# A routing search with its grids made in one instruction, and a weight's low half moved from TensorE and ScalarE to GpSimd

## The chip, the cores and the metric

The kernel runs on one core of a Trainium2 chip. The metric is the device time of one execution in microseconds. The engines are TensorE (PE in the rows; its weight loads are PEld), VectorE (DVE), ScalarE (ACT), GpSimd (POOL) and SyncE (SP), which issues most of the DMAs.

## The reference, cut to what matters

Three stages follow one another: attention that keeps the 32 best scores of a row, a mixture of eight experts with a capacity, and a rational activation between two products.

```python
def _moe_ref(x, w_gate, w1, w2):          # x: 2304 tokens x 512
    cap = N // E                          # 288 tokens for each of E = 8 experts
    logits = x @ w_gate
    order = np.argsort(-logits.flatten())
    for idx in order:                     # the best (token, expert) pairs first
        tok, e = int(idx) // E, int(idx) % E
        if assigned[tok] >= 0 or counts[e] >= cap:
            continue
        assigned[tok] = e
        counts[e] += 1
    ...
    for e in range(E):
        mask = assigned == e
        h = np.maximum(x[mask] @ w1[e], 0.0)
        out[mask] = h @ w2[e]

def _moe2_ref(x, w_in, w_out, a, b):
    h = x @ w_in
    P = a[0] + a[1] * h + a[2] * h**2 + a[3] * h**3
    Q = 1.0 + np.abs(b[0]) * np.abs(h) + np.abs(b[1]) * h**2
    return (P / (Q + 1e-06)) @ w_out
```

## The kernel before

**Stages.** The first 460 us are attention, 72 units of 128 rows by two heads, in an order written out by hand. Then comes routing, then the experts, eight in turn, each with two products (w1, w2) and the two of the rational stage (w_in, w_out).

**Weights.** The large products run in three half-precision passes, so every weight is split into a high half and a low half (`w1s`, `w2s`, `win`, `wout`). For w_in and w_out this takes several instructions: ScalarE makes "heads" (`heads`, L374 to L386), VectorE puts in the mantissa and the sign (`signed` L396, `mantissa` L409, `apply_sign` L413, in pieces of 256 columns), ScalarE sums squares (`square`, L307), and once a block's scale is known ScalarE makes the high half (L437) and VectorE the low one (L441). For the first expert's w1 and w2 (`add_first`) ScalarE makes the high half in four pieces of 1024 columns (`conv_hi`, L1361). The low half comes 256 columns at a time: TensorE multiplies the raw weights with a diagonal matrix that holds the scale (L1425) and subtracts the high half (L1426), and ScalarE copies the sum out of PSUM (L1429). There are 16 such pieces for w1 and 16 for w2. When the last is done, `stage` lets SP load four more raw pieces of w_out into the place that held the raw weights.

**Routing.** `route` replaces the sort by seven searches; each finds a threshold `edge` above which the next expert (or experts) fill up. A search has `ITS` = 4 iterations on a grid of `GR` = 32 thresholds, each grid 32 times finer than the last. In an iteration VectorE compares the 18 x 128 token values `vt` with the 32 thresholds `thr`, in two halves (`cmp`, L1493). TensorE counts how many tokens of each expert lie above each threshold, with 18 matmuls (L1501) and one for the need row (L1499, L1509 in the first iteration). VectorE makes `over`, which marks thresholds whose count reaches the need (L1565). TensorE adds `over` over the 32 thresholds and spreads the sum to all partitions (`pt`, L1569). VectorE makes the next grid from it:

```python
low = thr[:, 0:1] - step[:, it]                   # L1555, under the counts
nxt = iota_r * step[:, it + 1] + low              # L1558, under the counts
thr = step[:, it] * pb[:, 0:1] + nxt              # L1577, after the sum
```

After the fourth iteration VectorE makes `full` (which experts are full, L1582) and `edge` (L1583), masks the logits (`lc`, L1698), marks the tokens above the edge (`gone`, L1650) and starts the next search with `rng` (L1529) and its first grid `thr` (L1533). GpSimd multiplies the one-hot choice with `gone` (`asel`, or `asg` the first time; `give`, L1656), TensorE counts that with 18 matmuls (L1659), and the count goes into the `need` of the next search (L1671). GpSimd adds `asel` to `asg` (L1677).

**The order of the work around it.** Everything else is put between these instructions by a planner, `Flow`. It has a task for each piece of weight work, with an engine, a cost, the tasks that it needs and a rank. It keeps a clock for each engine and starts the task that can start first, ties by rank. `fill(n)` gives VectorE tasks of up to n us at a place in the program, and ScalarE, GpSimd and DMA tasks that by its clock start within 1.5 us (`LA`) of VectorE's. `tail(n)` gives TensorE up to n tasks. In each iteration there is a `fill` of 0.6 us under the counts (`J1`, `J3`), a `tail` of one task after the sum and a `fill` of 0.37 us (`J2`); between two searches a `tail` of one and a `fill(J4)` of 0. At the start of a search's last iteration GpSimd's clock is set 4.5 us ahead:

```python
if it == ITS - 1:
    flow.free["G"] = max(flow.free["G"], flow.free["V"] + 4.5)
```

No task on GpSimd was in those places before: `flow.add("G", ...)` stood only for the loads of an expert's rows and for the stores. Each engine runs its own instructions in program order and waits only for what they need.

After routing, `slots` and `rows_of` work out which rows go to which expert, a check sets a flag, and rows are gathered. If the flag is set, routing and all experts are run a second time by a slower path.

Of the kernel before, what the change touches and what calls it, by code (L numbers as in the profile page):

```python
# [8 lines left out]
F32 = mybir.dt.float32  # L9
BF16 = mybir.dt.bfloat16  # L10
# [5 lines left out]
OP = mybir.AluOpType  # L16
# [13 lines left out]
class Flow:  # L30
# [69 lines left out]
    def use(self, cost):  # L100
        self.free["V"] += cost
        return self.free["V"]
# [77 lines left out]
class Mark:  # L180
    end = None
# [3 lines left out]
def kernel(  # L185
# [62 lines left out]
    nc.vector.memset(onesb, 1.0)  # L248
    ones_row = consts.tile([1, P], F32, name="ones_row")
    nc.vector.memset(ones_row, 1.0)  # L250
    coef = consts.tile([P, 16], F32, name="coef")
# [11 lines left out]
    nc.gpsimd.iota(iota_r, pattern=[[1, GR]], base=0, channel_multiplier=0, allow_small_or_imprecise_dtypes=True)  # L263
    iota_f = consts.tile([P, GR], F32, name="iota_f")
    nc.vector.tensor_scalar(iota_f, iota_r, 1.001 / GR, None, op0=OP.mult)
    ITS, ITS_SLOW = 4, 7
    fine = consts.tile([P, ITS_SLOW], F32, name="fine")
    fine_slow = consts.tile([P, ITS_SLOW], F32, name="fine_slow")
    for i in range(ITS_SLOW):
        nc.vector.memset(fine[:, i : i + 1], 1.001 / GR ** (i + 1))  # L270
        nc.vector.memset(fine_slow[:, i : i + 1], 1.0 / (GR - 2) ** (i + 1))
# [204 lines left out]
    with ExitStack() as actx:  # L476
# [921 lines left out]
        def stage(which):  # L1398
# [11 lines left out]
            for i in range(4):  # L1410
                fetch((t[:, 1024 * i : 1024 * (i + 1)], -1, after), NP - 8 + 4 * (which - 1) + i)

        def add_first(which):

            scaled = add_steps(scale_steps(which, 0), [], -90.0)
            diag = npool.tile([P, P], F32, name=f"diag{which}", bufs=1)
            copies = [flow.add("A", 0.1, lambda: nc.scalar.activation(
# [40 lines left out]
        def routing(x, xs, lg, span, fast):  # L1458

            with ExitStack() as rctx:  # L1460
# [61 lines left out]
                def first_grid(slow, top):  # L1522

                    step = rw.tile([P, ITS_SLOW], F32, name="step")
                    rng = rw.tile([P, 1], F32, name="rng")
                    thr = rw.tile([P, GR], F32, name="thr")

                    def begin():
                        nc.vector.tensor_scalar(rng, top, span[:, 0:1], 1e-30, op0=OP.subtract, op1=OP.max)  # L1529

                    def middle():
                        if not slow:
                            nc.vector.tensor_scalar(thr, iota_f, rng, span[:, 0:1], op0=OP.mult, op1=OP.add)  # L1533

                    def end():
                        nc.vector.tensor_scalar(step, fine_slow if slow else fine, rng, None, op0=OP.mult)

                    return step, thr, begin, middle, end

                def search(edge, grid, vt, oh, need, fill, tail, use, until):  # L1540

                    step, thr = grid[0:2]
                    for it in range(ITS):
# [3 lines left out]
                        if it == 0:  # L1547
                            grid[4]()
                            need, rest = need()
                            compare(pc, need)  # L1550
                            rest()
                            use(0.4)
                        counts = use(C1) + 0.6
                        low = rw.tile([P, 1], F32, name="low")
                        nc.vector.tensor_tensor(low, thr[:, 0:1], step[:, it : it + 1], op=OP.subtract)  # L1555
                        if it < ITS - 1:
                            nxt = rw.tile([P, GR], F32, name="nxt")
                            nc.vector.tensor_scalar(  # L1558
                                nxt, iota_r, step[:, it + 1 : it + 2], low, op0=OP.mult, op1=OP.add
                            )  # L1560
                        use(0.28)
                        fill(J1 if it else J3)
                        until(counts)
                        over = rw.tile([GR, E + 1], BF16, name="over8")
                        nc.vector.tensor_scalar(  # L1565
                            over[:, 1:], pc, 0.0, None, op0=OP.is_ge, op1=OP.max, accum_out=over[:, 0:1]
                        )
                        pb = psr.tile([P, 512], F32, name="pt")[:, 0 : E + 1]
                        nc.tensor.matmul(pb, onesb[0:GR, :], over, start=True, stop=True)  # L1569
                        sums = use(0.07) + 0.36  # L1570
# [948 lines left out]
```

## Time and profile before

| | |
|---|---|
| three runs | 1209.81, 1213.32, 1213.90 us; median 1213.32 us |
| profiled execution | 1213.61 us, its span 1211.7 us |
| busy share of the span | PE 92%, DVE 87%, ACT 84%, POOL 32% |
| TensorE's mean granted clock | 0.929 |

Shares are averages over stages with different limits. The times below count from the first instruction of the profiled execution. Attention ends at about 460 us, the searches run to 545, slots and the gather to about 560, and the experts run to the end. In a row of the timeline the first number is the start, the second the duration in microseconds, then the engine, the line, the operation, what is written and read, the shapes, how many instructions the row stands for, and in brackets how long the engine had been idle before and what ended that.

### The profile page before, as it was taken

To read this page: it belongs to the slowest core of one execution; us is meant where nothing else is said; L and a number is where in the kernel's file an instruction comes from. 1 tells how busy PE (TensorE), PEld (TensorE's weight loads), DVE (VectorE), ACT (ScalarE), POOL (GpSimd) and SP (SyncE) were. 2 spreads that over 40 slices of the span, in tenths; PEclk is the share of its full clock that TensorE was granted. 3 is DMA by queue.
4 is the path that set the end of the run, shared out by engine and by line. 5 is a ranking of instruction groups with operands and counts; after the bars stand their busy time and mean duration, and the time that the engine had idled before them with its cause. 6 is when DMAs were issued, how large, how long until landed. Compare 5 with 4: busy or idle time off the path is not lost.

```text
span 1211.7 us, 26863 instructions
## 1 busy us (share of the span) xinstructions
PE 1117.0 (92%) x9716; PEld 903.7 (75%) x9716; DVE 1053.6 (87%) x4093; ACT 1020.0 (84%) x1816; POOL 385.3 (32%) x488
## 2 busy tenths in 40 slices
PE   5899999999999887885769999999999999999996
PEld 3688888888888765654546778888888888888774
DVE  5999999989889947888899789898989899897795
ACT  4999999999999796579999888888889888875684
POOL 3788888878777600003000010110100110001010
PEclk8899999999999985555989999999999999999998
DMA  5205102112000307412241302221311222000000
GB/s 126 52 10 160 45 22 52 27 44 52 2 2 2 140 1 289 150 54 89 72 159 71 139 27 84 90 90 71 98 51 52 90 90 84 8 1 21 1 22 22
DMA packets 81246, 80.62 MB, mean 67 GB/s; under 512 B 59984, under 2 KB 60112, under 8 KB 81104
## 3 DMA queue, kind: packets, MB, share of 16 engines
q1 hardware_dynamic: 78032, 69.34, 18.2%
q0 software_dynamic: 3072, 9.48, 2.7%
q8 instruction: 78, 1.28, 0.4%
q14 instruction: 64, 0.52, 0.1%
HBM read 69.25 MB, written 9.55 MB: 65 GB/s over the span
## 4 chain that ended last, share of the span: by engine, by line
PE 71%; DVE 14%; ACT 9%; issue 2%; POOL 1%; DMA 1%; SPq 0%; POOLq 0%; DVEq 0%; ACTq 0%
PE po L887 9%; PE s L696 6%; PE pt L855 5%; PE po L2017 4%; PE po L2018 4%; PE po L2016 4%; PE ph L2016 4%; PE pa L2016 4%; PE ph L2018 4%; PE ph L2017 4%; PE pa L2018 4%; PE pa L2017 4%; PE pt L859 3%; PE po L891 2%; PE pl L1425 2%
## 5 line engine op out<-in xcount | busy, mean ns | idle before, releaser
L789 POOL TENSOR_TENSOR win<-sv,sg 128x576 f32<-128x576 f32 x142 | 179.1, 1282 | 64.4 <-ACT sg L784 47.2
L753 DVE MAX8 cd<-sv 128x8 f32<-128x82 f32 (+1 forms) x1008 | 178.1, 229 | 11.0 <-ACT sv L706 10.9
L2016 PE MATMUL ph<-x,win 128*128 128x288 f16 x512 | 148.3, 290 | 7.6 <-DVE uv L2285 7.5
L887 PE MATMUL po<-vm,pT 128*128 128x65 f32 (+1 forms) x1280 | 152.4, 267 | 2.1 <-issue 1.1
L2017 PE MATMUL po<-g,wout 128*128 128x288 f16 x512 | 146.4, 286 | 2.3 <-DVE g L2007 2.3
L2017 PE MATMUL ph<-x,win 128*128 128x288 f16 x512 | 148.3, 290 | 0.0
L2018 PE MATMUL ph<-x,win 128*128 128x288 f16 x512 | 148.1, 289 | 0.0
L2016 PE MATMUL po<-g,wout 128*128 128x288 f16 x512 | 146.4, 286 | 1.4 <-ACT g L2006 1.3
L2018 PE MATMUL po<-g,wout 128*128 128x288 f16 x512 | 146.4, 286 | 0.0
L887 PEld LDWEIGHTS po<-vm,pT 128*128 128x128 f32 (+1 forms) x1280 | 140.2, 183 | 5.1 <-issue 2.1
L855 PE MATMUL pt<-ident,sv 128*128 128x128 f32 x648 | 125.8, 283 | 0.3 <-ACT pT L869 0.3
L859 PE MATMUL pt<-dg,mk 128*128 128x128 bf16 x720 | 120.0, 220 | 1.2 <-POOL mk L846 1.2
L1993 POOL DMA_INDIRECT xe<-xrows,rows_i x24 | 28.5, 1189 | 286.2 <-PE pa L2028 266.0
L2276 ACT ACTIVATE z<-ph,inv 128x288 f32<-128x288 f32 x128 | 63.6, 497 | 57.9 <-PE ph L2018 54.9
L784 ACT ACTIVATE sg<-sv,cut_all 128x576 bf16<-128x576 f32 x142 | 109.0, 777 | 3.8 <-DVE cut_all L759 3.8
L2406 POOL DMA_INDIRECT out_dram<-ob,tok x21 | 23.2, 1105 | 277.2 <-ACT ob L2402 223.0
L845 ACT ACTIVATE sg<-sv,pn 128x576 bf16<-128x576 f32 x136 | 97.8, 770 | 13.5 <-POOL pn L823 13.5
L696 PE MATMUL s<-region 64*128 64x288 f32 (+1 forms) x640 | 95.3, 451 | 13.1 <-ACT region L667 9.0
L790 DVE MAX8 w<-win 128x8 f32<-128x576 f32 x142 | 105.4, 743 | 0.0
L855 PEld LDWEIGHTS pt<-ident,sv 128*128 128x128 f32 x648 | 92.7, 143 | 15.6 <-ACT sg L784 3.8
L846 POOL TENSOR_SCALAR mk<-sg 128x576 bf16<-128x576 bf16 x136 | 88.8, 671 | 1.8
L706 ACT ACTIVATE sv<-s 128x1152 f32<-128x1152 f32 x72 | 80.5, 1117 | 5.6 <-PE s L696 3.5
(367 smaller groups left out, 3315.4 us busy)
## 6 DMA issues: line engine op xcount, KB each, us to landing
region<-in_moe_w_dram SPq DMA_DIRECT2D x16, 2048.0 KB, 8.3
xrows<-x SPq DMA_DIRECT2D x1, 4644.0 KB, 22.0
region<-in_q_dram SPq DMA_DIRECT2D x32, 128.0 KB, 3.0
region<-in_k_dram SPq DMA_DIRECT2D x32, 128.0 KB, 2.9
vm<-in_v_dram SPq DMA_DIRECT2D x32, 128.0 KB, 3.1
wout<-in_moe_w_in_dram SPq DMA_DIRECT2D x8, 511.8 KB, 7.8
region<-in_moe_w_out_dram SPq DMA_DIRECT2D x8, 511.8 KB, 3.6
win<-in_moe_w_in_dram SPq DMA_DIRECT2D x6, 511.8 KB, 7.6
```

Of the source, the lines that this page charges most:

```text
L696: nc.tensor.matmul(sc[p0 : p0 + n, 2 * hh + g, 0:w], qT[rows, j, p0 : p0 + n], kT[rows, bb, c : c + w], start=True, stop=True,)
L753: nc.vector.max(cd[:, g, :], sv[:, o : o + n])
L784: nc.scalar.activation(sg, sv_t[u, hh], AF.Sign, bias=cut_all[:, 2 * u + hh, 7:8], scale=-OVER, accum_out=t["sum"][:, c : c + 1],)
L789: nc.gpsimd.tensor_tensor(win, sv_t[u, hh], sg, op=OP.mult)
L790: later.append(lambda c=c, win=win: nc.vector.max(t["w8"][:, c, :], win))
L845: nc.scalar.activation(sg, sv, AF.Sign, bias=t["pn"][:, c : c + 1])
L855: nc.tensor.transpose(dst, pr[:, c * P : (c + 1) * P], ident)
L859: nc.tensor.matmul(dst, mk_buf[u % 2][:, o : o + P], bat[b]["dg"][:, 2 * i + hh, :], start=False, stop=True, skip_group_check=True,)
L887: nc.tensor.matmul(po[p0 : p0 + n, i, hh, :], sb[:, hh * (R + 1) + c, p0 : p0 + n], vm[:, bb, hh, c, :], start=(c == 0), stop=False,)
L2016: nc.tensor.matmul(acc, ah, bh, start=first, stop=False)
L2017: nc.tensor.matmul(acc, ah, bl, start=False, stop=False)
L2018: nc.tensor.matmul(acc, al, bh, start=False, stop=last)
```

## The change

Four things change.

- The four grids of a search are prepared in one instruction: `base` holds (j + 1) / 32^(i+1) times the range plus the lower end, for all four i. `low`, `nxt` and `step` go. The later grids are `rng * pb + base[it + 1]`.
- TensorE adds up the marks with weights 32^-(i+1). In iteration `it` it first adds the marks of the iterations before again, into the same PSUM tile, and then those of this iteration, so that `pb` holds the position found so far. `edge` is worked out from it once, and `full` marks the experts whose whole position is that of the largest. `over8` has four buffers.
- The planner is no longer told of 0.28 us for `low` and `nxt`.
- For the first expert's w2 the low half is made by GpSimd, 256 columns at a time, in two instructions each, 32 in all: it multiplies the raw weights by their scale in place and subtracts the high half. The products on TensorE, the diagonal matrix and ScalarE's copies for w2 go. w1 stays as it was.

```diff
-    ones_row = consts.tile([1, P], F32, name="ones_row")
-    nc.vector.memset(ones_row, 1.0)
+    ones_row = ones[0:1, :]
-    iota_f = consts.tile([P, GR], F32, name="iota_f")
-    nc.vector.tensor_scalar(iota_f, iota_r, 1.001 / GR, None, op0=OP.mult)
-    fine = consts.tile([P, ITS_SLOW], F32, name="fine")
+    grids = consts.tile([P, ITS, GR], F32, name="grids")
+    weights = consts.tile([GR, ITS], BF16, name="weights")
+    for i in range(ITS):
+        nc.vector.tensor_scalar(grids[:, i, :], iota_r, 1.0, float(GR) ** -(i + 1), op0=OP.add, op1=OP.mult)
+        nc.vector.memset(weights[:, i : i + 1], float(GR) ** -(i + 1))
...
+        def scaled_raw(o):
+            w = w_raw[2, 0][:, o]
+            nc.gpsimd.tensor_tensor(w, w, w_scale[2, 0][0].to_broadcast([P, 256]), op=OP.mult)
+
+        def rest_of(o):
+            h, l = w_split[2, 0]
+            nc.gpsimd.tensor_tensor(l[:, o], w_raw[2, 0][:, o], h[:, o], op=OP.subtract)
+
         def add_first(which):
 
             scaled = add_steps(scale_steps(which, 0), [], -90.0)
+            if which == 2:
+                done = []
+                for c in range(4):
+                    t = flow.add("A", 0.95, lambda c=c: conv_hi(2, 0, c), [scaled], -88.0)
+                    for o in range(c * 1024, (c + 1) * 1024, 256):
+                        t = flow.add("G", 0.65, lambda o=o: scaled_raw(slice(o, o + 256)), [t], -88.0)
+                        t = flow.add("G", 0.65, lambda o=o: rest_of(slice(o, o + 256)), [t], -89.0)
+                    done.append(t)
+                return flow.add("A", 0.0, lambda: stage(2), done, -90.0)
...
                     def begin():
-                        nc.vector.tensor_scalar(rng, top, span[:, 0:1], 1e-30, op0=OP.subtract, op1=OP.max)
+                        if slow:
+                            nc.vector.tensor_scalar(rng, top, span[:, 0:1], 1e-30, op0=OP.subtract, op1=OP.max)
+                        else:
+                            nc.vector.tensor_scalar(rng, top, span[:, 0:1], 1.001, op0=OP.subtract, op1=OP.mult)
 
                     def middle():
                         if not slow:
-                            nc.vector.tensor_scalar(thr, iota_f, rng, span[:, 0:1], op0=OP.mult, op1=OP.add)
+                            nc.vector.tensor_scalar(base, grids, rng, span[:, 0:1], op0=OP.mult, op1=OP.add)
...
+                    def spread(pb, i, last):
+                        nc.tensor.matmul(
+                            pb, weights[:, i : i + 1].to_broadcast([GR, P]), overs[i], start=(i == 0), stop=last
+                        )
...
                         counts = use(C1) + 0.6
-                        low = rw.tile([P, 1], F32, name="low")
-                        nc.vector.tensor_tensor(low, thr[:, 0:1], step[:, it : it + 1], op=OP.subtract)
-                        if it < ITS - 1:
-                            nxt = rw.tile([P, GR], F32, name="nxt")
-                            nc.vector.tensor_scalar(
-                                nxt, iota_r, step[:, it + 1 : it + 2], low, op0=OP.mult, op1=OP.add
-                            )
-                        use(0.28)
+                        pb = psr.tile([P, 512], F32, name="pt")[:, 0 : E + 1]
+                        for i in range(it):
+                            spread(pb, i, False)
                         fill(J1 if it else J3)
                         until(counts)
-                        over = rw.tile([GR, E + 1], BF16, name="over8")
+                        over = rw.tile([GR, E + 1], BF16, name="over8", bufs=ITS)
...
-                        pb = psr.tile([P, 512], F32, name="pt")[:, 0 : E + 1]
-                        nc.tensor.matmul(pb, onesb[0:GR, :], over, start=True, stop=True)
+                        overs.append(over)
+                        spread(pb, it, True)
...
                             nc.vector.scalar_tensor_tensor(
-                                thr, step[:, it : it + 1].to_broadcast([P, GR]), pb[:, 0:1], nxt, op0=OP.mult, op1=OP.add
+                                thr, rng.to_broadcast([P, GR]), pb[:, 0:1], base[:, it + 1, :], op0=OP.mult, op1=OP.add
                             )
...
-                            nc.vector.tensor_scalar(edge, step[:, it : it + 1], pb[:, 0:1], low, op0=OP.mult, op1=OP.add)
+                            nc.vector.tensor_scalar(edge, rng, pb[:, 0:1], span[:, 0:1], op0=OP.mult, op1=OP.add)
```

## Rows read from the trace of the kernel before

**Rows 1.** Stretches: length, busy PE, PEld, DVE, ACT, POOL; granted clock, DMA share, GB/s.
```profile
500.00:520.00 20.00, 17.84 (x191) 11.94 (x190) 17.29 (x82) 15.37 (x26) 0.89 (x2) 0.50 0.13 42
...
558.00:572.00 14.00, 6.64 (x29) 4.31 (x29) 13.96 (x44) 12.47 (x23) 5.92 (x5) 0.50 0.26 65
```

**Rows 2.** Timeline of TensorE, one iteration of the third search.
```profile
489.85 0.16 PE L1569 MATMUL pt<-over,onesb 32*128 32x9 bf16 x1 [0.26 <-DVE over L1565]
489.94 1.22 PE L1425 MATMUL pl<-region,diag 128*128 128x256 f32 x2
...
491.51 0.64 PE L1501 MATMUL pl<-oh,cmp 128*32 128x8 bf16 x18
492.41 0.16 PE L1569 MATMUL pt<-over,onesb 32*128 32x9 bf16 x1 [0.26 <-DVE over L1565]
```

**Rows 3.** Timeline of VectorE: end of the second search, an iteration of the third.
```profile
482.26 0.16 DVE L428 TENSOR_REDUCE nq<-nq 128x1 f32<-128x4 f32 x1 [0.96 <-ACT junk L307]
...
490.06 0.25 DVE L1577 SCALAR_TENSOR_TENSOR thr<-step,pt,nxt 128x32 f32<-128x32 f32 x1
490.34 0.83 DVE L1493 TENSOR_TENSOR cmp<-vt,thr 128x288 bf16<-128x288 f32 x2
491.09 0.15 DVE L1555 TENSOR_TENSOR low<-thr,step 128x1 f32<-128x1 f32 x1
...
491.49 0.42 DVE L413 TENSOR_TENSOR win<-win 128x256 f32<-128x256 f32 x1
492.19 0.16 DVE L1565 TENSOR_SCALAR_CACHE_REDUCE over<-pl 32x8 bf16<-32x8 f32 x1 [0.29 <-PE pl L1501]
...
492.28 0.43 DVE L396 SCALAR_TENSOR_TENSOR ring<-wout,ring 128x256 uint16<-128x256 uint16 x1
492.62 0.25 DVE L1577 SCALAR_TENSOR_TENSOR thr<-step,pt,nxt 128x32 f32<-128x32 f32 x1
```

**Rows 4.** Timeline of VectorE, an iteration of the first search without a product.
```profile
464.40 0.25 DVE L1577 SCALAR_TENSOR_TENSOR thr<-step,pt,nxt 128x32 f32<-128x32 f32 x1
...
466.42 0.26 DVE L1577 SCALAR_TENSOR_TENSOR thr<-step,pt,nxt 128x32 f32<-128x32 f32 x1 [0.19 <-PE pt L1569]
```

**Rows 5.** Line L1429: ns min/median/max, first and last start in us.
```profile
L1429 ACT ACTIVATE w1s<-pl x16: 348/384/385, 472.7 to 508.5; 128x256 f16<-128x256 f32 x16
L1429 ACT ACTIVATE w2s<-pl x16: 349/384/476, 509.6 to 547.0; 128x256 f16<-128x256 f32 x16
```

**Rows 6.** Timeline of VectorE, `need` of the sixth search and after the last.
```profile
523.45 0.17 DVE L1671 TENSOR_TENSOR need<-cb,pt 128x8 f32<-128x8 f32 x1 [1.02 <-PE pt L1659]
...
547.45 0.16 DVE L1671 TENSOR_TENSOR need<-cb,pt 128x8 f32<-128x8 f32 x1 [0.86 <-PE pt L1659]
```

**Rows 7.** Timeline of VectorE, GpSimd and ScalarE around changes of search.
```profile
462.18 0.17 DVE L1640 TENSOR_TENSOR vt<-top,pen 128x18 f32<-128x18 f32 x1
...
471.66 0.43 POOL L1656 TENSOR_TENSOR asg<-oh,gone 128x144 bf16<-128x144 bf16 x1 [9.49 <-DVE gone L1650]
...
473.24 1.14 ACT L1361 ACTIVATE w2s<-region,ws 128x1024 f16<-128x1024 f32 x1
...
496.63 0.46 POOL L1677 TENSOR_TENSOR asg<-asg,asel 128x144 bf16<-128x144 bf16 x1
...
496.70 0.41 DVE L1640 TENSOR_TENSOR vt<-top,pen 128x18 f32<-128x18 f32 x1
```

**Rows 8.** Timeline of VectorE and GpSimd at the end of attention.
```profile
412.55 0.79 DVE L830 TENSOR_SCALAR mk<-sv,tau_all 128x576 bf16<-128x576 f32 x1
...
412.55 2.24 DVE L830 TENSOR_SCALAR mk<-sv,tau_all 128x576 bf16<-128x576 f32 x2
...
412.98 2.95 POOL L1090 TENSOR_TENSOR win<-sv,sg 128x576 f32<-128x576 f32 x2
...
422.22 0.51 DVE L830 TENSOR_SCALAR mk<-sv,tau_all 128x576 bf16<-128x576 f32 x1
```

**Rows 9.** GpSimd's groups by form: count, busy us, mean ns, idle before.
```profile
L789 POOL TENSOR_TENSOR win<-sv,sg 128x576 f32<-128x576 f32 x142 | 179.1, 1282 | 64.4 <-ACT sg L784 47.2 <-DVE cd L753 15.6 <-DVE den L905 1.6
```

More of the change, by code (lines that the diff above doesn't have):

```diff
@@ L263 @@
     nc.gpsimd.iota(iota_r, pattern=[[1, GR]], base=0, channel_multiplier=0, allow_small_or_imprecise_dtypes=True)
-    iota_f = consts.tile([P, GR], F32, name="iota_f")
-    nc.vector.tensor_scalar(iota_f, iota_r, 1.001 / GR, None, op0=OP.mult)
     ITS, ITS_SLOW = 4, 7
-    fine = consts.tile([P, ITS_SLOW], F32, name="fine")
+    grids = consts.tile([P, ITS, GR], F32, name="grids")
+    weights = consts.tile([GR, ITS], BF16, name="weights")
     fine_slow = consts.tile([P, ITS_SLOW], F32, name="fine_slow")
+    for i in range(ITS):
+        nc.vector.tensor_scalar(grids[:, i, :], iota_r, 1.0, float(GR) ** -(i + 1), op0=OP.add, op1=OP.mult)
+        nc.vector.memset(weights[:, i : i + 1], float(GR) ** -(i + 1))
     for i in range(ITS_SLOW):
-        nc.vector.memset(fine[:, i : i + 1], 1.001 / GR ** (i + 1))
         nc.vector.memset(fine_slow[:, i : i + 1], 1.0 / (GR - 2) ** (i + 1))
@@ L1522, in first_grid @@
                 def first_grid(slow, top):
-                    step = rw.tile([P, ITS_SLOW], F32, name="step")
                     rng = rw.tile([P, 1], F32, name="rng")
-                    thr = rw.tile([P, GR], F32, name="thr")
+                    if slow:
+                        step = rw.tile([P, ITS_SLOW], F32, name="step", bufs=1)
+                    else:
+                        base = rw.tile([P, ITS, GR], F32, name="base", bufs=1)
                     def begin():
-                        nc.vector.tensor_scalar(rng, top, span[:, 0:1], 1e-30, op0=OP.subtract, op1=OP.max)
+                        if slow:
+                            nc.vector.tensor_scalar(rng, top, span[:, 0:1], 1e-30, op0=OP.subtract, op1=OP.max)
+                        else:
+                            nc.vector.tensor_scalar(rng, top, span[:, 0:1], 1.001, op0=OP.subtract, op1=OP.mult)
                     def middle():
                         if not slow:
-                            nc.vector.tensor_scalar(thr, iota_f, rng, span[:, 0:1], op0=OP.mult, op1=OP.add)
+                            nc.vector.tensor_scalar(base, grids, rng, span[:, 0:1], op0=OP.mult, op1=OP.add)
                     def end():
-                        nc.vector.tensor_scalar(step, fine_slow if slow else fine, rng, None, op0=OP.mult)
-                    return step, thr, begin, middle, end
+                        if slow:
+                            nc.vector.tensor_scalar(step, fine_slow, rng, None, op0=OP.mult)
+                    return step if slow else rng, None if slow else base, begin, middle, end
                 def search(edge, grid, vt, oh, need, fill, tail, use, until):
-                    step, thr = grid[0:2]
+                    rng, base = grid[0:2]
+                    thr, overs = base[:, 0, :], []
+                    def spread(pb, i, last):
+                        nc.tensor.matmul(
+                            pb, weights[:, i : i + 1].to_broadcast([GR, P]), overs[i], start=(i == 0), stop=last
+                        )
                     for it in range(ITS):
@@ L1547, in search @@
                         if it == 0:
-                            grid[4]()
                             need, rest = need()
```

## The prediction

> **What bounds the kernel now.** I began with the page's forty slices and went to the table by stretches, since the change touches one stretch only. Between attention and the experts lie routing, to 546 us, and the slots of the rows, to 558. There TensorE runs at the lower of its two levels (granted clock 0.50): only small matmuls are left, and it idles between them [rows 1]. From 558 to 572 VectorE is 100% busy and sets the end, ScalarE has gaps [rows 1]. So time won or lost in routing moves everything behind it, while ScalarE work taken away there is worth little.
>
> Routing is seven searches of four iterations. An iteration is one loop: VectorE compares (`cmp`), TensorE counts, VectorE makes `over`, TensorE adds it up (`pt`), VectorE makes the next `thr`. From the timeline of TensorE the reader is to see what stands in that loop: behind `pt` comes a product for an expert's low half (L1425, 1.22 us, and L1426), then the need row, the 18 counts, and `pt` again 2.56 us after the last one [rows 2]. The counts start when the product is through, not when `cmp` is. The same loop seen from VectorE: `over` waits 0.29 us for the counts although two pieces of weight conversion (L413, L396) stand in it [rows 3]. An iteration without a product, in the first search, takes 464.40 to 466.42: 2.02 us [rows 4]. So a product costs 0.54 us per iteration, and `low` and `nxt` cost nothing where one runs: they lie under the counts.
>
> **The change part by part.**
>
> *Searches 5 to 7 lose their products.* The 16 copies of the first w1 end at 508.5, the 16 of w2 run from 509.6 to 547.0 [rows 5], one product per iteration and one per change of search. These searches are the last three. Nine iterations fall from 2.56 to about 2.03 (the two conversion pieces still fit: from `cmp` to the second one's end VectorE is busy 0.75 + 0.34 + 0.09 + 0.34 us, `thr` 0.28 more, 1.80 in all): 4.8 us. The three first iterations lose `step`, `low` and `nxt` on VectorE (0.40 us from `low` to the first piece [rows 3], and `step`) and a product ahead of the counts; between 0 and 0.5 us each, I take 0.3, since the need row then limits: 0.9. The one wait of 1.02 us for a late count at 523.45 goes: 1.0 [rows 6]. Together 6.7 us. After the last search `need` waits 0.86 us for a count that stood behind two products [rows 6]; the new count can start when GpSimd's mask is there, 0.5 of it goes. First iterations of searches 2 to 4: 0.3 each, 0.9. Sum of the gains so far 8.1 us.
>
> *Constants, bases, extra sums.* Fewer small memsets at the start lie under the first loads: nothing. `base` has 128 columns where the first `thr` had 32. A like instruction takes 0.51 us for 576 columns [rows 8], so 96 more cost 0.09 us at most; seven of them 0 to 0.6, I take 0.4. The sums of earlier grids are up to three tiny matmuls behind the counts, 0.09 us each from `pt` to the product behind it [rows 2]; TensorE waits 0.26 us there for `over` [rows 2], which hides them. If it did not, 6 x 0.09 x 7 = 3.8 us.
>
> *ScalarE and the DMAs.* 16 copies of 0.384 us go [rows 5], 6.1 us, and w2's four piece loads on SP's queue, which wait for the last low half, are issued some 40 us earlier. SP has only a few loads behind them, and they bring forward ScalarE's conversions at 547 to 560. I count this at nothing: VectorE bounds 558 to 572 [rows 1]. If ScalarE did bound, up to 3 us could be won.
>
> *32 instructions on GpSimd.* This term decides. Alone, a product over 128x576 takes 1.282 us [rows 9]. What happens beside VectorE is in two places. `vt`, 18 columns with two inputs in SBUF, starts at 496.70 inside GpSimd's `asg` and ends with it: 0.41 us where it took 0.17 with GpSimd quiet [rows 7]. At 412.55 masks, 0.51 us each when alone, meet two GpSimd products: the first mask ends at 413.34, the second only at 414.79 [rows 8]. They take strict turns: the second mask ran after the first product, the second product after that mask. From the second mask's end (414.79) to the second product's (412.98 + 2.95 = 415.93) GpSimd held for 1.14 us. Scaled by 256/576 one of the new instructions holds 0.50 us, with 0.14 of start 0.65 alone.
>
> The Trainium skill (SBUF — State Buffer, Who interferes with whom) says that a VectorE instruction with two SBUF inputs and a GpSimd instruction that reads SBUF exclude one another for a whole instruction. The trace agrees, with the 0.41 us above; taken as 32 whole instructions of 0.65 us it gives the top of the dear rival below, 1225.8 us.
>
> How many turns? The planner lets GpSimd run 1.5 us ahead of its clock, reserves it from the last iteration on for `asel`, and knows nothing of turns: by its costs (0.65 + 0.07 each, 7.7 us open per search) it queues about 12 in search 2, 12 in search 3, 8 in search 4. The chip starts each as soon as the one ahead is through. So they run five to an iteration: VectorE's two halves of `cmp`, two pieces and `thr` all have two SBUF inputs. Such an iteration takes 5 x 0.50 of GpSimd, 1.33 of VectorE (0.33, 0.33, 0.30, 0.30, 0.07) and 0.15 before GpSimd's first: 3.98 us in place of 2.56, 0.28 per instruction. In a first iteration no product hides them: 0.36. Ten of these and 22 of the others: 9.8 us. In search 2 VectorE waits 0.96 us for ScalarE anyway [rows 3]; 0.9 comes off. From both sides: nothing, if all fall into waits; 0.65, the whole instruction, 20.8 us. I take 0.31 on average, near the turns of [rows 8], which are the nearest rows. What is queued behind them on GpSimd is `asel`, for which the next counts' need waits; twelve turns of 0.84 us last 10 us and a search 12 or more, so it is not late.
>
> Sum against the profiled execution, 1213.61 us (span 1211.7 and 1.9 around it; 0.3 above the median shown): -8.1 - 0.9 + 0.4 + 9.8 = +1.2, **1214.8 us**. With c the price of one GpSimd instruction the change is 32c - 8.6: it breaks even at 0.27 us. Clear of 0.3% (3.6 us, about what a measurement of this kernel can tell from no change) it is faster below 0.16 and slower above 0.38.
>
> **The rivals.**
> *Turns in the waits (faster).* Place: searches 2 to 4. VectorE has 0.29 us idle in an iteration and gains 0.40 [rows 3], room for one turn of 0.50. If GpSimd's instructions come one or two to an iteration, or if VectorE keeps its turn over several instructions, c falls to 0 to 0.16 and the gains stand: 1205.0 to 1210, 1208 in the middle. For: a product of TensorE hides what VectorE loses there. Against: nothing spaces the queue, and [rows 8] show strict turns. It decides below 0.16.
> *Whole price (slower).* If every instruction holds up VectorE for its length, c is 0.38 to 0.65: 1217.2 to 1225.8, 1221 in the middle. For: VectorE is busy most of routing, and a late `cmp` makes the counts late as well. Against: the products' 0.54 us per iteration are slack in just these searches.
> *`asel` behind the queue (slower).* If the planner puts the first GpSimd instruction ahead of search 1's `asel`, that waits for w2's first high half (done at 474.38) and does not start at 471.66 [rows 7]: 2.7 us more, 1217.5 or a little above. By its costs that misses by 0.3 us.
> *The fast path fails.* Edges are rounded otherwise than thresholds; if a row falls between, the flag is set and routing and experts run again: some 650 us more, the time from 558 to the end.
> *No change at all* is the first case by another way: gains and turns cancel.
>
> **How the numbers follow.** The sum, with c from 0.16 to 0.38: 0.43, and its own range is 1210 to 1217. Turns in the waits 0.27; whole price 0.23; `asel` late 0.05; fast path fails 0.02. So faster 0.27, same 0.43, slower 0.30. The range takes in the middle of both sides and the bounds of the small terms: 1206 to 1223.
>
> **What the profile after would show.** `thr` to `thr` of 2.0 to 2.1 us in searches 5 to 7: the gain is right. 32 GpSimd instructions of 0.5 to 0.9 us between about 474 and 515, in three bunches, and iterations of about 4 us with `cmp` halves of 0.8 to 1 us where 0.45 is usual: the turns are right. If the bunches are loose, or `cmp` keeps its length, the price is wrong and the kernel is faster; if `asel` starts over 0.5 us after `gone`, or iterations pass 4.5 us, it is slower. ScalarE bounding 558 to 572 would show that I wrongly counted its relief at nothing.

## The result

| | before | after |
|---|---|---|
| runs | 1209.81 to 1213.90 us, median 1213.16 us (4) | 1221.21 to 1224.70 us, median 1221.89 us (4) |
| profiled execution, span | 1211.7 us | 1220.6 us |
| TensorE's mean granted clock | 0.929 | 0.929 |

The ratio is 1.0085, interval 1.0070 to 1.0101: the kernel became slower by 0.85%, where I forecast 1214.8 us and no measurable change. The medians differ by 8.7 us. That the time lies in my range is luck: it got there for reasons that I did not have.

Where the time went shows best by place. The table gives, from VectorE's timeline of each profile, the time from the start of routing's work (the copy to `lc`) to `full`, which ends the first search, then from one `full` to the next; "rest" is the span from the result of the flag's test (`unusual`) to the end. Attention ends up to 4 us earlier or later from one profile to another, so spans are not to be compared, stretches are.

| us | search 1 | 2 | 3 | 4 | 5 | 6 | 7 | `full` to `unusual` | rest |
|---|---|---|---|---|---|---|---|---|---|
| before | 10.18 | 12.34 | 12.04 | 12.00 | 12.14 | 13.11 | 12.14 | 12.96 | 654.2 |
| after | 9.90 | 14.98 | 15.05 | 12.91 | 10.20 | 11.19 | 15.47 | 12.23 | 659.2 |

Searches 2 to 4 lose 6.6 us, where GpSimd's instructions are. Searches 5 and 6 win 3.9, but search 7 loses 3.3 where it should have won 2. And the rest, which holds no line that the change touches, is 5.0 us longer.

The stretches of the profile after that answer to [rows 1]:

```profile
500.00:520.00 20.00, 16.74 (x211) 11.45 (x210) 17.79 (x77) 14.61 (x22) 5.80 (x9) 0.50 0.46 158
...
558.00:572.00 14.00, 4.89 (x31) 3.36 (x29) 12.78 (x41) 10.01 (x21) 3.83 (x4) 0.50 0.15 42
```

From 558 to 572 VectorE is no longer always busy: routing ends at 561.4 there, not at 557.5. The clock is at its lower level, 0.50, in these stretches of both kernels, so it explains nothing there.

**The turns.** VectorE's timeline after, an iteration of search 2 (its counterpart is the iteration in [rows 3]):

```profile
473.51 0.65 DVE L1601 SCALAR_TENSOR_TENSOR thr<-rng,pt,base 128x32 f32<-128x32 f32 x1
474.20 1.59 DVE L1510 TENSOR_TENSOR cmp<-vt,thr 128x288 bf16<-128x288 f32 x2
475.71 0.89 DVE L413 TENSOR_TENSOR win<-win 128x256 f32<-128x256 f32 x1
476.52 0.15 DVE L1589 TENSOR_SCALAR_CACHE_REDUCE over<-pl 32x8 bf16<-32x8 f32 x1
...
476.61 0.80 DVE L413 TENSOR_TENSOR win<-win 128x256 f32<-128x256 f32 x1
477.33 0.60 DVE L1601 SCALAR_TENSOR_TENSOR thr<-rng,pt,base 128x32 f32<-128x32 f32 x1
```

GpSimd's timeline of the same kernel, its first bunch and the `asel` behind it:

```profile
472.65 0.66 POOL L1415 TENSOR_TENSOR region<-region,ws 128x256 f32<-128x256 f32 x1 [1.98 <-ACT w2s L1361]
473.39 0.73 POOL L1419 TENSOR_TENSOR w2s<-region,w2s 128x256 f16<-128x256 f32 x1
474.08 1.40 POOL L1415 TENSOR_TENSOR region<-region,ws 128x256 f32<-128x256 f32 x2
...
481.61 1.50 POOL L1419 TENSOR_TENSOR w2s<-region,w2s 128x256 f16<-128x256 f32 x2
485.21 0.43 POOL L1680 TENSOR_TENSOR asel<-oh,gone 128x144 bf16<-128x144 bf16 x1 [2.09 <-DVE gone L1674]
```

The reader is to see that every VectorE instruction with two SBUF inputs grows by 0.35 to 0.48 us (`thr` from 0.25, the two halves of `cmp` from 0.83 together, the pieces from 0.41), while `over`, which reads PSUM, keeps its 0.15. The iteration takes 3.82 us, and five GpSimd instructions fit in it. `asel` is not late.

**The searches without a product.** VectorE, an iteration of search 5:

```profile
518.45 0.25 DVE L1601 SCALAR_TENSOR_TENSOR thr<-rng,pt,base 128x32 f32<-128x32 f32 x1
518.73 0.83 DVE L1510 TENSOR_TENSOR cmp<-vt,thr 128x288 bf16<-128x288 f32 x2
...
520.48 0.25 DVE L1601 SCALAR_TENSOR_TENSOR thr<-rng,pt,base 128x32 f32<-128x32 f32 x1
```

2.03 us, as worked out. But VectorE waits for ScalarE in search 6 (1.12 us) and stops in search 7 (5.32 us), and both waits are new:

```profile
515.36 0.14 DVE L1326 COPY x_max<-pa 128x1 f32<-128x1 f32 x1
...
530.90 0.45 DVE L396 SCALAR_TENSOR_TENSOR ring<-wout,ring 128x256 uint16<-128x256 uint16 x1 [1.12 <-ACT ring L378]
...
536.71 0.15 DVE L1708 TENSOR_TENSOR left<-left,pt 128x8 f32<-128x8 f32 x1
542.18 0.16 DVE L428 TENSOR_REDUCE nq<-nq 128x1 f32<-128x4 f32 x1 [5.32 <-ACT junk L307]
```

ScalarE's timeline says why it was late. L384 to L386 are the heads (the first three steps of a weight piece's conversion) of the eight pieces that are loaded over the first expert's raw weights:

```profile
511.39 1.33 ACT L384 ACTIVATE region<-region 128x512 int8<-128x512 bf16 x1
512.75 1.34 ACT L385 ACTIVATE region<-region 128x512 bf16<-128x512 bf16 x1
514.13 0.76 ACT L386 ACTIVATE region<-region,bias 128x512 uint32<-128x512 uint16 x1
...
538.62 0.74 ACT L386 ACTIVATE region<-region,bias 128x512 uint32<-128x512 uint16 x1
539.27 0.64 ACT L307 ACTIVATE junk<-wout 128x512 bf16<-128x512 f32 x1
...
541.42 0.63 ACT L307 ACTIVATE junk<-wout 128x512 bf16<-128x512 f32 x1
```

From 511 to 539 most of ScalarE's time goes into such heads; the planner counts 0.52, 0.52 and 0.61 us for the three, the chip takes 1.33, 1.34 and 0.75. The sum of squares (L307) for which `nq` waits comes behind them. In the kernel before the heads of the last four pieces start at 547.3, behind the searches. SP's timeline of these loads, before (the last one into w1's place and the four into w2's) and then after (all eight):

```profile
508.32 38.77 SPq L341 DMA_DIRECT2D region<-in_moe_w_out_dram  x5
```

```profile
483.14 30.64 SPq L341 DMA_DIRECT2D region<-in_moe_w_out_dram  x8
```

Each load waits for the low halves of its own 1024 columns. Before, the four into w2's place are issued at 517.9, 528.5, 538.0 and 546.8 us, one by one; after, at 483.1, 488.7, 503.0 and 505.4. The planner, which counts on them from w2's last low half on, now puts all eight pieces' heads into the searches. Line L384, eight heads, before and then after (ns min/median/max, first and last start in us):

```profile
L384 ACT ACTIVATE region<-region x8: 1317/1332/1405, 509.9 to 556.5; 128x512 int8<-128x512 bf16 x8
```

```profile
L384 ACT ACTIVATE region<-region x8: 1323/1394/1420, 511.4 to 532.4; 128x512 int8<-128x512 bf16 x8
```

### The profile page after: what moved, and what is told of

It is laid out like the page before. It is cut to its first block, busy times and chain, and to the rows that moved or that the text cites. A ratio compares the mean times of both kernels' runs of the same rounds, so it can differ in the third digit from the quotient of the medians.

```text
span 1220.6 us, 26812 instructions
## 1 busy us (share of the span) xinstructions
PE 1099.5 (90%) x9710; PEld 892.3 (73%) x9710; DVE 1057.7 (87%) x4036; ACT 1014.5 (83%) x1799; POOL 406.2 (33%) x520
## 4 chain that ended last, share of the span: by engine, by line
PE 59%; DVE 21%; ACT 12%; issue 3%; POOL 3%; DMA 0%; SPq 0%; POOLq 0%; DVEq 0%; ACTq 0%
PE po L887 6%; PE ph L2040 4%; PE ph L2042 4%; PE ph L2041 4%; PE po L2041 4%; PE po L2042 4%; PE po L2040 4%; PE s L696 4%; PE pa L2040 4%; PE pa L2042 4%; PE pa L2041 4%; PE pt L855 3%; DVE cd L753 3%; PE pt L859 2%; DVE w L790 2%
## 5 line engine op out<-in xcount | busy, mean ns | idle before, releaser
L2017 POOL DMA_INDIRECT xe<-xrows,rows_i x24 | 24.3, 1013 | 296.0 <-PE pa L2052 275.8
L696 PE MATMUL s<-region 64*128 64x288 f32 (+1 forms) x640 | 92.7, 439 | 16.5 <-ACT region L667 12.5
L869 ACT ACTIVATE pT<-pt 128x1152 f32<-128x1152 f32 x72 | 81.5, 1132 | 3.5 <-PE pt L859 3.3
```

The lines of the kernel that those rows point to most:

```text
L696: nc.tensor.matmul(sc[p0 : p0 + n, 2 * hh + g, 0:w], qT[rows, j, p0 : p0 + n], kT[rows, bb, c : c + w], start=True, stop=True,)
```

## The experiments

Three theories stood at first. A: the turns on GpSimd cost what the change wins elsewhere, and more. B: the early loads fill ScalarE, and VectorE waits for it in the last search. C: the planner's clock, without the 0.28 us for `low` and `nxt`, orders the work behind routing worse. X and L, on the rest, came later.

Each kernel of an experiment was timed in five rounds beside the kernel before, whose median was 1212.4 to 1212.8 us there; the row of the kernel after is that of the result, four runs. The runs of one kernel spread over 3 to 7 us, and the stretches are each read from one profile. "2 to 4" and "5 to 7" are sums of searches, worked out like the table above.

| | median us | ratio, interval | 2 to 4 | 5 to 7 | rest |
|---|---|---|---|---|---|
| before | 1212.7 | | 36.38 | 37.39 | 654.2 |
| after | 1221.89 | 1.0085, 1.0070 to 1.0101 | 42.94 | 36.86 | 659.2 |
| e1_search_only | 1211.79 | 0.9986, 0.9974 to 0.9999 | 35.82 | 36.79 | 653.1 |
| e2_gpsimd_only | 1223.91 | 1.0097, 1.0079 to 1.0116 | 46.43 | 37.51 | 659.8 |
| e3_late_loads | 1215.92 | 1.0026, 1.0014 to 1.0038 | 42.94 | 30.68 | 657.0 |
| e4_no_gpsimd | 1213.92 | 1.0014, 1.0003 to 1.0025 | 35.57 | 36.89 | 657.1 |
| e5_late_loads_late_x | 1213.92 | 1.0015, 1.0003 to 1.0028 | 42.71 | 32.06 | 655.8 |
| e6_late_loads_no_gpsimd | 1209.99 | 0.9979, 0.9967 to 0.9992 | 35.55 | 30.70 | 659.1 |
| e7_true_costs | 1217.30 | 1.0045, 1.0029 to 1.0062 | 42.94 | 32.86 | 656.4 |
| e8_all_three | 1207.92 | 0.9964, 0.9948 to 0.9979 | 36.18 | 32.09 | 656.0 |
| e9_half_the_turns | 1210.30 | 0.9980, 0.9970 to 0.9990 | 39.37 | 32.08 | 655.4 |
| e10_low_on_vector | 1216.53 | 1.0030, 1.0017 to 1.0042 | 35.99 | 31.49 | 664.9 |
| e11_spread_turns | 1211.89 | 0.9998, 0.9987 to 1.0008 | 36.70 | 33.57 | 658.4 |

### Which half of the change: e1, e2

e1 is the kernel after with w2's low half made as before:

```diff
-            if which == 2:
+            if False:
```

> The new search with w2's low half made as before (products on TensorE, copies on ScalarE). Theory A (GpSimd's turns with VectorE made the loss) and theory B (w2's four raw pieces come early, their heads fill ScalarE, and VectorE's fill in the last search waits for it) both have nothing to act on here: first iterations 0.3 us shorter in six searches, 1 to 3 us under the kernel before, 1210 to 1213 us. Theory C (the planner's clock without its 0.28 us puts the work behind routing in a worse order) says 3 to 6 us over the kernel before, 1216 to 1219 us.

e2 is the kernel before with the new `add_first`, `scaled_raw` and `rest_of` alone.

> The old search with GpSimd making the low half of w2. Theory A: what the products give back in searches 5 to 7 (about 6 us) against turns in searches 2 to 4 (about 8 us) and no gain in the first iterations: 1214 to 1217 us. Theory B: the same early loads as in the changed kernel, so its stall of 5 us in the last search and the 5 us behind routing stand: 1221 to 1226 us. Theory C: without the shorter planner clock no loss behind routing, 1214 to 1218 us.

The new search alone wins 1 to 2 us, GpSimd's half alone costs 11; e1 came out as theories A and B have it, e2 in theory B's band and above theory A's. With e1's rest at 653.1 us the planner's missing 0.28 us does no harm behind routing: that theory (C) is refuted. In the old search the 32 instructions cost 46.43 - 36.38 = 10.05 us, 0.31 each; this price is less sure than those below, since e2's profile is of a run of 1229.31 us, 5.4 above that kernel's median.

### Early loads or turns: e3, e4

e3 holds back, in the planner's clock, the loads over w2's raw weights until the last search has been laid out:

```diff
+        release = Mark()
...
-                return flow.add("A", 0.0, lambda: stage(2), done, -90.0)
+                return flow.add("A", 0.0, lambda: stage(2), done + [release], -90.0)
...
+                        if ph == E - 2 and not slow:
+                            release.end = flow.free["V"]
```

> The changed kernel, with the loads of w2's four raw pieces held until the last search, where they stood before. Theory A: turns in searches 2 to 4 as before, so 1219 to 1223 us. Theory B: no wait of over 2 us of VectorE for ScalarE's squares in the last search, the stretch behind routing back to that of the kernel before; 8 to 11 us under the changed kernel, 1211 to 1214 us. Theory C: the wait goes (5 us), the 5 us behind routing stay, 1216 to 1218 us.

e4 keeps the order and the planner's costs, with `scaled_raw` and `rest_of` empty and the first expert's low half of w2 set to zero ahead of routing.

> The changed kernel by the same plan, but GpSimd's 32 instructions are left out (the low half of the first expert's w2 is zeros, set ahead of routing): no turns, everything else in the same order. Theory A: cmp halves of 0.45 us, searches 2 to 4 shorter by 7 to 9 us in sum and the whole by as much, 1212 to 1215 us. Theory B: searches 2 to 4 shorter too, but ScalarE's heads are as many and have less time, so VectorE's wait in the last search grows by most of it, and the whole stays at 1218 to 1222 us.

Both causes are there, in separate places. e3 brings searches 5 to 7 to 30.68 us, 6.7 below the kernel before, and the kernel 6.0 us down. Its time lies between theory B's band and theory C's: the waits go, but 2.8 us stay behind routing. On the chip the loads are not held that long. SP's timeline in e3, the last load into w1's place and w2's four:

```profile
513.25 2.33 SPq L341 DMA_DIRECT2D region<-in_moe_w_out_dram  x5
```

SP issues them by 515.6 us, 27 us before search 7 ends, and the waits are gone all the same. What e3 moves is the place of these pieces' heads in ScalarE's queue: four of the eight now start at 542.4 to 551.6, at the end of search 7 and behind it. So it is the planned place of the heads that counts, and not only when the data come. e4, in theory A's band, takes 7.4 us out of searches 2 to 4 and keeps the wait in search 7, with no GpSimd instruction left that could make it:

```profile
534.98 0.16 DVE L428 TENSOR_REDUCE nq<-nq 128x1 f32<-128x4 f32 x1 [5.34 <-ACT junk L307]
```

Both leave the rest at 657, 3 us above the kernel before, where the kernel after has 659.2.

### The rest, and whether the causes add up: e5 to e8

What differs in all of these from e1 is x's scale. Its chain (the maximum of all of x, then `s_x`) has rank -85 in the planner, behind w1's and w2's products with -88. With w2's 16 products gone it is done at 515, inside search 5 (`x_max`, above), not at 558 as before. e5 is e3 with that chain held back too:

```diff
-            [], -85.0,
+            [release], -85.0,
```

> The changed kernel with w2's four piece loads held back to the end of the last search (as in e3_late_loads), and x's scale chain held back to the same point, where the kernel before had it. It tests what makes the stretch behind routing 3 us longer (657.0 and 657.1 us from the end of routing to the end in e3 and e4, 654.2 before). Theory X, the small steps of x's scale take slots of searches in which weight pieces ran before: one more piece is done by the end of routing, the stretch falls to about 654, and the kernel to 1212.5 to 1213.5, about 3 us below e3's 1215.9. Theory L, the order of loads behind routing makes it, whatever runs in routing's slots: 657 stays, 1215.5 to 1216.5.

e6 is e3 and e4 together; e8 is e5 and e4 together.

> The changed kernel with w2's loads held back and the 32 GpSimd instructions left out (the low half of the first w2 is zero, so that part of the products is missing). If the turns (7.4 us in searches 2 to 4, e4) and the wait in the last search (6 us, e3) are separate causes, they add up: 1221.9 - 6.0 - 8.0, 1207.5 to 1209. If they are one cause told twice (the searches' slack takes up one when the other goes), 1211 or more. Searches: 10.2 or less each in the last three, below 12.1 in searches 2 to 4, 76 to 77 us in all.

> Late loads, late scale chain of x, and none of the 32 GpSimd instructions (the low half of the first w2 is zero, so that part is missing): all three causes taken away. If they are separate and all of the loss, the time is that of the kernel before less the searches' gains of 8 us: 1204.5 to 1206.5. With theory L in place of X: 1207.5 to 1209, as e6.

e7 is the kernel after with another planner's cost for the heads, and nothing else:

```diff
-                    t = [flow.add("A", (0.52, 0.52, 0.61)[k], lambda n=n, k=k: heads(n)[k][2](), t, rank + 0.5, late)]
+                    t = [flow.add("A", ((0.52, 0.52, 0.61), (1.1, 1.1, 0.75))[n >= NP - 8][k], lambda n=n, k=k: heads(n)[k][2](), t, rank + 0.5, late)]
```

> The changed kernel as it is, but the planner counts the heads of the last eight weight pieces (ScalarE, strided writes) at 1.1, 1.1 and 0.75 us, where it had 0.52, 0.52 and 0.61. Theory B, the loads' early arrival fills ScalarE with work that the planner takes for half as long, and the norm's sum in the last search is put too near: with the true costs that wait of 5.3 us goes, last search 10.2 to 11.5 in place of 15.5, time 1215.5 to 1218. Rival, ScalarE is simply too full there, and the same work is late wherever it is planned: 1220 to 1223. It can also lose behind routing, if the heads are put off.

e7 settles most of the wait in search 7: the same loads, the same heads, but planned nearer to what they take (1.1, 1.1 and 0.75 us for 1.33, 1.34 and 0.75), and the kernel falls by 4.6 us. Searches 5 and 6 take 10.2 us each. What is left of the wait is

```profile
538.06 0.16 DVE L428 TENSOR_REDUCE nq<-nq 128x1 f32<-128x4 f32 x1 [2.27 <-ACT junk L307]
```

so I had the last search, 12.4 us, about 1 us too low. So 3.0 of the 5.3 us, and the 1.1 in search 6, were a matter of order: `nq` stands in VectorE's queue where the planner believed the sum ready, and all of the search stands behind it.

e5 shows what x's chain does. Its small steps take slots in which pieces of weights ran: of the groups L409 and L396 one pair less is through by the end of routing. L409 up to there, after and then e5 (x16 in the kernel before too):

```profile
L409 DVE SCALAR_TENSOR_TENSOR wout<-wout,ring x15: 407/409/737, 499.1 to 548.8; 128x256 uint32<-128x256 uint32 x15
```

```profile
L409 DVE SCALAR_TENSOR_TENSOR wout<-wout,ring x16: 408/410/741, 498.4 to 542.7; 128x256 uint32<-128x256 uint32 x16
```

And the wait of TensorE's first products of the experts for VectorE's `uv`, from 560 to 720 us, in the table of waits (total, times, longest), before, after and e5:

```profile
PE ph L2016 <- DVE uv L2285: 4.9, 6, 1.7
```

```profile
PE ph L2040 <- DVE uv L2309: 14.7, 5, 6.4
```

```profile
PE ph L2044 <- DVE uv L2313: 4.8, 5, 2.6
```

In e3, e4, e6 and e7, all with the early chain, it is 12.4 to 14.5 us. By the medians the kernel wins 2.0 us by e5 over e3 and 2.1 by e8 over e6, much less than that wait falls. The profiles show less still: what the rest wins (1.2 and 3.1 us) the searches lose in part, 1.4 us in search 6 of both to a wait for an `nq` and 0.6 in search 2 of e8, so that outside attention e5 is 0.1 us shorter than e3 and e8 1.2 shorter than e6. e5 lies between the bands of the two theories, e8, at 1207.92, misses the 1204.5 to 1206.5 of all causes taken away and lies in the band that I gave to theory L. So theory X is supported in kind and not settled. e6 came out 1 us above what I gave for it: its searches are as short as expected, but its rest, 659.1 us, is that of the kernel after and not the 657 of e3 and e4.

The rest falls into groups, and so does TensorE's granted clock behind the flag's test. The stretches from 15 to 30 us and from 90 to 105 us behind the flag's test, before and then after:

```profile
572.50:587.50 15.00, 13.65 (x110) 10.68 (x109) 13.01 (x30) 14.19 (x25) 3.03 (x1) 0.98 0.65 218
647.50:662.50 15.00, 15.00 (x125) 12.04 (x124) 14.79 (x33) 14.69 (x27) 0.00 (x0) 1.00 0.37 141
```

```profile
576.40:591.40 15.00, 14.72 (x111) 11.29 (x110) 12.99 (x30) 14.48 (x25) 0.00 (x0) 0.91 0.53 202
651.40:666.40 15.00, 13.94 (x95) 10.21 (x95) 10.58 (x26) 11.08 (x22) 0.00 (x0) 0.79 0.55 203
```

In these two stretches e2 and e6 have the clocks of the kernel after (rest 659.1 to 659.8), e3, e4 and e7 have 0.98 to 1.00 and 0.89 (656.4 to 657.1), e5, e8 and e9 0.87 to 0.93 and 1.00 (655.4 to 656.0), and e1 0.97 and 1.00 (653.1). e10 and e11, treated below, do not fit in: 0.96 and 0.77 (664.9), 0.95 and 1.00 (658.4). Whether the clock makes the rest longer or only follows TensorE's waits no run separates, and why the rest stays 1 to 2 us above the kernel before in e5, e8 and e9 stays open.

### Number and spacing of the turns: e9 to e11

All three are e5 with another way to make w2's low half. e9 lets ScalarE scale the raw weights, so that 16 GpSimd instructions are left:

```diff
         def scaled_raw(o):
             w = w_raw[2, 0][:, o]
-            nc.gpsimd.tensor_tensor(w, w, w_scale[2, 0][0].to_broadcast([P, 256]), op=OP.mult)
+            nc.scalar.activation(w, w, AF.Copy, scale=w_scale[2, 0][0])
...
+                    t = flow.add("A", 0.95, lambda c=c: scaled_raw(slice(c * 1024, (c + 1) * 1024)), [t], -88.0)
                     for o in range(c * 1024, (c + 1) * 1024, 256):
-                        t = flow.add("G", 0.65, lambda o=o: scaled_raw(slice(o, o + 256)), [t], -88.0)
```

> As e5_late_loads_late_x, but ScalarE scales the raw w2 in place (four instructions of 128x1024), so that GpSimd has 16 subtractions left in place of 32 instructions. In e5 searches 2 to 4 take 42.7 us, in e8 without any GpSimd instruction 36.2, so 32 of them cost 6.5 us. If the price goes by the number of turns, 16 cost 3.3: searches 2 to 4 take 39.4 and the kernel 1213.9 - 3.3, about 1210.6, below the kernel before. Rival, the price is the length of the bunches on VectorE whatever their number, or ScalarE's added 4 us make GpSimd and the other pieces late: 41 us or more in searches 2 to 4, 1212.5 to 1214.

e10 makes it on VectorE, in one instruction for each 256 columns:

```diff
+            nc.vector.scalar_tensor_tensor(
+                l[:, o], w_raw[2, 0][:, o], w_scale[2, 0][0], h[:, o], op0=OP.mult, op1=OP.subtract
+            )
```

> As e5_late_loads_late_x, but VectorE makes the low half itself, 16 instructions of 128x256 with scale and subtraction in one, and GpSimd none. It shows what the same work costs on the engine that the turns are taken from. 16 of about 0.33 us are 5.3 us; VectorE's idle 0.3 to 0.4 us in an iteration with a product hides part. Theory, VectorE's time in searches 2 to 4 sets the price: 2 to 5.3 us over e8 (36.2), so 38 to 41.5 us in searches 2 to 4, 1210 to 1213 in all. If GpSimd's turns were the cheaper way, over 1214.

e11 scales on VectorE and spaces the subtractions:

```diff
-                        t = flow.add("G", 0.65, lambda o=o: scaled_raw(slice(o, o + 256)), [t], -88.0)
-                        t = flow.add("G", 0.65, lambda o=o: rest_of(slice(o, o + 256)), [t], -89.0)
-                    done.append(t)
+                        t = flow.add("V", 0.22, lambda o=o: scaled_raw(slice(o, o + 256)), [t] + done, -88.0)
+                        t = flow.add("G", 1.9, lambda o=o: rest_of(slice(o, o + 256)), [t], -89.0)
+                        done = [t]
```

> As e9, 16 GpSimd subtractions, but VectorE scales each piece of 128x256 right ahead (0.22 us), and each piece is planned 1.9 us after the one before, so that GpSimd has about one instruction in an iteration, three in a search, and never a queue. It tests whether a turn alone is cheaper than a turn in a bunch. Rival of the prediction (turns in the waits): an instruction that comes alone falls where VectorE waits, costs 0 to 0.16, and only VectorE's 16 x 0.22 = 3.5 us are seen, less in searches 2 to 4: 1209 to 1211.5. Theory of strict turns: it holds up one VectorE instruction by up to 0.5 us wherever it falls, and in searches 5 to 7, where VectorE sets the pace, all of that is paid: 1213 to 1216.

e9 came out as expected to 0.3 us. Against e8 searches 2 to 4 cost 6.5 us with 32 instructions (e5) and 3.2 with 16: 0.20 each in both. This version makes the whole of the reference's output and beats the kernel before by 0.20% (interval 0.10 to 0.30%), the kernel after by 11.6 us. Its GpSimd instructions still stand in a bunch:

```profile
475.72 2.93 POOL L1421 TENSOR_TENSOR w2s<-region,w2s 128x256 f16<-128x256 f32 x4 [3.92 <-ACT region L1417]
478.83 6.26 POOL L1421 TENSOR_TENSOR w2s<-region,w2s 128x256 f16<-128x256 f32 x8 [0.18 <-ACT region L1417]
...
487.12 3.40 POOL L1421 TENSOR_TENSOR w2s<-region,w2s 128x256 f16<-128x256 f32 x4
```

In e11 a turn comes alone. VectorE's timeline with GpSimd's instruction, an iteration of search 2 with a product and one of search 5 without:

```profile
476.49 0.26 DVE L1603 SCALAR_TENSOR_TENSOR thr<-rng,pt,base 128x32 f32<-128x32 f32 x1
476.58 0.70 POOL L1421 TENSOR_TENSOR w2s<-region,w2s 128x256 f16<-128x256 f32 x1 [2.45 <-DVE region L1417]
476.78 1.18 DVE L1512 TENSOR_TENSOR cmp<-vt,thr 128x288 bf16<-128x288 f32 x2
...
479.06 0.25 DVE L1603 SCALAR_TENSOR_TENSOR thr<-rng,pt,base 128x32 f32<-128x32 f32 x1
...
510.25 0.26 DVE L1603 SCALAR_TENSOR_TENSOR thr<-rng,pt,base 128x32 f32<-128x32 f32 x1
510.33 0.70 POOL L1421 TENSOR_TENSOR w2s<-region,w2s 128x256 f16<-128x256 f32 x1 [2.27 <-DVE region L1417]
510.54 1.18 DVE L1512 TENSOR_TENSOR cmp<-vt,thr 128x288 bf16<-128x288 f32 x2
...
512.64 0.25 DVE L1603 SCALAR_TENSOR_TENSOR thr<-rng,pt,base 128x32 f32<-128x32 f32 x1
```

`cmp` grows by 0.35 us in both. Beside a product the iteration still takes 2.57 us: the turn is free. Without one it takes 2.39 instead of 2.03: all of it is paid. That is the mechanism of my rival "turns in the waits", and it was right to ask for spacing. The time, 1211.89, lies between the two bands that I gave: the one mechanism holds beside a product, the other without. Searches 2 to 7 cost 70.27 - 68.27 = 2.0 us more than in e8, for 16 turns and 16 VectorE instructions. Yet e11 is slower than e9, and e10, whose searches are as short as if the low half were free, is slower still. L409 up to the end of routing in e10:

```profile
L409 DVE SCALAR_TENSOR_TENSOR wout<-wout,ring x8: 407/410/420, 515.8 to 535.0; 128x256 uint32<-128x256 uint32 x8
```

Eight in place of 16, and of L396 10 in place of 17: 16 instructions for w2 pushed 15 pieces of other weights out of routing's slots, and the rest grew by 10.7 us over the kernel before. In e11 it is 4 of L409 and 5 of L396, and 4.2 us. I had looked for e10's price in searches 2 to 4 (38 to 41.5 us, and 1210 to 1213 in all); they take 36.0, and the price lies behind routing. That the pieces pushed out make it is read from these counts; no run shows it by itself.

## Why the prediction was wrong

- *Searches 5 to 7, 6.7 us: right.* e3 measures 37.39 - 30.68 = 6.7, with iterations of 2.03 us. In the kernel after the wait in search 7 took it back.
- *Last count, 0.5: right.* `full` to `unusual` falls by 0.7.
- *Constants, bases, extra sums, first iterations: right within what can be told.* With neither turns nor the new wait, searches 2 to 4 take 35.57 (e4) where they took 36.38: 0.8 less, for 0.9 less what `base` costs.
- *The turns: right in form, too dear by a fifth.* Bunches from 472.7 to 505.4, strict turns, five to an iteration, `asel` in time: all as forecast. The iteration takes 3.8 us, not 3.98. After against e4 the 32 instructions cost 7.4 us (0.23 each), where I had 8.9, that is 9.8 less 0.9 for the wait in search 2. By the Trainium skill (SBUF — State Buffer, Who interferes with whom) the engine that comes second waits until the first one's instruction is through. The traces agree that it waits: in e11 a lone GpSimd instruction of 0.70 us that began 0.20 us before `cmp` delayed it by 0.35, less than the 0.50 that were left of it. None of the turns shown cost the whole 0.65.
- *"ScalarE and the DMAs. I count this at nothing": this step failed.* I saw that w2's four loads would come 40 us earlier and bring ScalarE's conversions forward, and asked only whether ScalarE's relief would help behind routing. I did not ask where the conversions would go: into searches 5 to 7, whose shorter iterations have less time for them, ahead of the squares that a VectorE `nq` waits for. Waits of 5.3 and 1.1 us in searches 7 and 6 are what they cost there. Price in the whole, by e3: 6.0 us, and without the turns (e4 to e6) 3.9. e7, whose loads come as early, shows that the planner's too low costs put `nq` there. e3 shows that data which are issued 27 us before the end of search 7 cost nothing in the searches where their heads are queued behind it.
- *The products on TensorE: one effect missed.* I counted what the loop wins when they go, not which task of lower rank moves up in their place. x's scale chain did, and took slots from weight pieces: 2 us of the kernel's time by the medians of e5 and e8, 1.2 to 3.1 of the rest, but only 0.1 and 1.2 of the whole outside attention by their profiles.
- *Rivals.* "Whole price" gives 1221 us, close to the result, by a mechanism that did not happen: its price of 0.38 to 0.65 is refuted by 0.20 to 0.23. "`asel` late" and "fast path fails" did not come about. None of the rivals ended a search in a wait for ScalarE.

With the two missed terms, 1214.8 + 6.0 + 2, less the 1.5 by which I had the turns too dear, the sum is 1221.3 us against 1221.89. That it agrees so closely is partly luck. By place the profile of the kernel after has 10.0 us more outside attention than the one before, half of it in the rest, and of these 5.0 us late heads take back 2.2 (e3) and x's late chain 1.2 more (e5); the last 1.6 are not explained.

## What to carry to other kernels

When a change frees a buffer or an engine, follow what moves up: the loads that the buffer releases, the work that these trigger, and the next task by rank on the freed engine; then ask which in-order queue meets that work too early. A planner that fills gaps by a table of costs must have the costs of the forms that really run (here 1.33 us stood as 0.52), since one instruction queued before its input is ready stops everything behind it. Work put into another engine's gaps can be paid where the pushed-out work lands, so compare the whole time, not the stretch: e10 had almost the shortest searches and a slower kernel.

## What the runs showed of the hardware

- GpSimd's two-input instructions on 128x256 take 0.61 to 0.99 us beside a busy VectorE (after and e5), and 0.67 to 0.78 alone (e11). In a bunch they cost searches 2 to 4 0.20 us each, 32 of them (e5) as well as 16 (e9), and 0.23 and 0.31 in other surroundings (after, e2); alone, beside a product of TensorE, nothing that can be seen in the iteration (2.57 us, e11).
- ScalarE takes 1.33 us for 128x512 where it writes a one- or two-byte element into every 8 bytes (L384, L385), and 0.76 where it writes four-byte elements at the same spacing (L386). With the function and the spaced input of L385, but a two-byte element written into every 4 bytes, it takes 0.77 (L374).
